# Bucketed attention and two expert stages on one core: the order of the queries, and the maxima over two PSUM banks

## The chip, the cores and the metric

The kernel runs on one core of a Trainium2 chip. The metric is the device time of one execution in microseconds (us); lower is better. TensorE (PE in the profile) multiplies matrices, its weight loads (PEld) overlap its multiplications, VectorE is DVE, ScalarE is ACT, GpSimd is POOL, and SyncE (SP) only issues DMAs here. PSUM, into which TensorE writes, has 8 banks of 512 fp32 numbers per partition.

## The reference

Three stages follow one another: an attention in which a query sees only the keys of its own bucket, a layer of 8 experts with one expert per token, and a dense layer with a gated product. Only the first matters here.

```python
def _attn_ref(q, k, v, proj):            # q, k, v: 2 x 8 x 768 x 64
    q_bits = einsum(q, proj) > 0         # 6 bits per row; the same for k
    mask = q_bucket == k_bucket
    scores = where(mask, q @ k.T / sqrt(D), -1e9)
    attn = exp(scores - max(scores)); attn /= attn.sum() + 1e-9
    return attn @ v
```

## The kernel before

**Layout.** There are 16 heads (2 batches of 8) of 768 queries and keys, NC = 6 chunks of P = 128 each; HS = 384 is half a head. Every engine gets its instructions in the order in which the program is written, and works through them in that order; a wait of one instruction holds all that stand behind it on its engine. For each head there is a set of four SBUF tiles X, Y, K1, K2 (`sets`, four sets in turn). X holds 64 rows of the scaled queries, 12 rows of bucket bits (64 to 75) and, in row 76, the maximum of each query; K2 holds the same for the keys, with -1 in row 76. Y and K1 hold the other halves of a split of the fp32 numbers. So one product of X and K2 over 77 rows gives score, mask and minus the maximum in one go.

**Steps.** The attention runs over 96 steps, one per head and chunk of keys. Step k does, in this order: the work that is due (`due(k - 0.5)`), a fp16 copy of the exponentials of the step before (`high`), `scores(k)` (four matmuls of 384 columns, L402 and L403, and two exponentials, L404), the rest of the split (`low`, mostly on GpSimd), the maxima of a chunk of queries eight steps ahead (`mx(k + 8)`), in every odd step the products with the values of two steps (`pv`, 36 matmuls, L430 to L432), and what else is due. `later` is a table of due times with the constants of `Q`: preparing a head (`prep`, about 13 steps ahead; its DMAs go through SP's queue), the bits of four heads (`bits`), scaling the values (`vmax`, `vscale`, `vsplit`), and dividing the finished sums (`evac`, at the begin of the step after a head's last `pv`; the next head's first `pv` ends the step after that one).

**Maxima.** `mx` multiplies a chunk of queries (the stationary operand, 76 rows and 128 columns of X) with all keys of K2, 384 columns at a time, each into a PSUM tile of one bank (`ps_m`, three tiles), and VectorE reduces each half to one number per query. The queries of chunk c are the columns c, c + 6, c + 12 and so on (`c::NC`), so that partition p gets queries 6p to 6p + 5. After the sixth chunk a reduction (L391) takes the larger half and -0.5 as a floor; `top[:, h]`, 128 partitions of 6 numbers, is then written by a DMA (L392) as 768 numbers into row 76 of X. The sixth chunk of head h is sent in step 6h - 3, and `scores(6h)` is the first that reads the row.

**Sums.** `pv` adds into a PSUM tile of one bank per head (`ps_v`, two tiles in turn). `scores` uses two banks (`ps_t`), small things one (`ps_x`): eight in all.

**Start.** Before step 0 the first head's bits are computed (two tiles of `ps_m`, L667), then its six chunks of maxima; after the sixth chunk the first two of the eight dot products for the bits of heads 0 to 3 (`bits(0)`, L358, into two tiles of `ps_v`), four filling matmuls (`heat`), the maxima of the values on VectorE (L514), a transposition for their scale (L531), the other dot products, and the first scores.

Of the kernel before, what the change touches and what calls it, by code (L numbers as in the profile page):

```python
# [9 lines left out]
F32 = mybir.dt.float32  # L10
F32R = mybir.dt.float32r
F16 = mybir.dt.float16
I32 = mybir.dt.int32
AF = mybir.ActivationFunctionType
# [37 lines left out]
def moe_attention_kernel(ctx, tc, qk, v, vt, pj, wg, w1, w2, win, wout, out, cap):  # L52
# [5 lines left out]
    def opened(stack, name, bufs, side="left", **kw):  # L58
        return stack.enter_context(tc.tile_pool(name=name, bufs=bufs, side=side, reuse_waits="tile", **kw))

    def f32(t):
        return t.bitcast(F32)
# [201 lines left out]
    with ExitStack() as actx:  # L264
# [2 lines left out]
        ph = opened(actx, "ph", 1)  # L267
        pt = opened(actx, "pt", 2)
        ps_t = opened(actx, "ps_t", 2, space=PSUM)
        ps_m = opened(actx, "ps_m", 3, space=PSUM)  # L270
        ps_v = opened(actx, "ps_v", 2, space=PSUM)
        ps_x = opened(actx, "ps_x", 1, space=PSUM)

        idle_sb = pa.tile([P, 512], F16, tag="idle", name="idle_sb")
# [15 lines left out]
        ]  # L290
        warm = pa.tile([1, 1], F32, tag="warm", name="warm")
        pool.memset(b3, 3.0)
        rt, b_t = {}, {}
        nm = pa.tile([P, NH, NC], F32, tag="nm", name="nm")
        top = pa.tile([P, NH, NC], F32R, tag="top", name="top")
        mxs = [pa.tile([P, NC, 3], F32, tag=f"mx{i}", name=f"mx{i}") for i in range(2)]
        for t in mxs:
            dve.memset(t[:, :, 2:3], -0.5)
        nflag = pa.tile([1, NH // 2 + 1], I32, tag="nflag", name="nflag")
        pf_t, phi_t, plo_t, pv_t, xp_t = {}, {}, {}, {}, {}  # L300
        vr_t, vt_t, vh_t, am_t, sc_t, sw_t = {}, {}, {}, {}, {}, {}
# [8 lines left out]
        def prep(h, first=False):  # L310

            st = sets[h % 4]
            r = rt[h]
            if h == 1:
                hi = pt.tile([P, S], F32, tag="pf", name=f"hi{h}", bufs=4).bitcast(F32R)
            else:
                hi = ph.tile([P, S], F32R, tag="hi", name=f"hi{h}", bufs=1)
            lo = ph.tile([P, S], F32R, tag="lo", name=f"lo{h}")
            act.activation(hi, r, AF.Copy, scale=SC)
            if not first:  # L320
                sp.dma_start(out=f32(st["X"])[0:D], in_=f32(hi)[0:D])
                sp.dma_start(out=f32(st["K2"])[0:D], in_=f32(hi)[D:P])
            if h == 1:
                yield
            sp.dma_start(out=f32(st["K1"])[0:D], in_=f32(hi)[D:P])
            sp.dma_start(out=f32(st["Y"])[D:P], in_=f32(hi)[0:D])
            yield
            if h > 2:
                put_bits(h)
            if h in Q["ap"]:  # L330
                x = pt.tile([P, S], F32, tag="pf", name=f"rs{h}", bufs=4) if h < 2 else r
                act.activation(x, r, AF.Copy, scale=SC)
                pool.tensor_tensor(out=lo, in0=x, in1=f32(hi), op=ALU.subtract)
            else:
                dve.scalar_tensor_tensor(out=lo, in0=r, scalar=SC, in1=f32(hi), op0=ALU.mult, op1=ALU.subtract)
            sp.dma_start(out=f32(st["K1"])[D:P], in_=f32(lo)[D:P])
            sp.dma_start(out=f32(st["Y"])[0:D], in_=f32(lo)[0:D])

        def put_bits(h):
            st = sets[h % 4]  # L340
            b = b_t[h // 4]
            o = 32 * (h % 4)
            sp.dma_start(out=f32(st["X"])[D : D + 12], in_=f32(b)[o : o + 12])
            sp.dma_start(out=f32(st["K2"])[D : D + 12], in_=f32(b)[o + 12 : o + 24])
# [34 lines left out]
        def mx(n):  # L379
            h, c = divmod(n, NC)  # L380
            st = sets[h % 4]
            mm = mxs[h % 2]
            for n in range(2):
                ps = ps_m.tile([P, 512], F32, tag="m", name=f"psm{h}{c}{n}")
                pe.matmul(  # L385
                    ps[:, :HS], st["X"][0:76, c::NC], st["K2"][0:76, n * HS : (n + 1) * HS], start=True, stop=True
                )
                dve.tensor_reduce(out=mm[:, c, n : n + 1], in_=ps[:, :HS], axis=AX.X, op=ALU.max)  # L388
            if c == NC - 1:

                dve.tensor_reduce(out=top[:, h], in_=mm, axis=AX.X, op=ALU.max)  # L391
                sp.dma_start(out=f32(st["X"])[76:77, :].rearrange("o (p c) -> o p c", c=NC), in_=f32(top)[:, h])  # L392

        def scores(k):
            h, j = divmod(k, NC)
            st = sets[h % 4]
            pf = pf_t[k] = pt.tile([P, S], F32, tag="pf", name=f"pf{k}", bufs=4)
            kc = slice(j * P, (j + 1) * P)
            for n in range(2):
                ps = ps_t.tile([P, 512], F32, tag="t", name=f"pst{k}{n}")  # L400
                qc = slice(n * HS, (n + 1) * HS)
                pe.matmul(ps[:, :HS], st["K1"][:, kc], st["Y"][:, qc], start=True, stop=False)  # L402
                pe.matmul(ps[:, :HS], st["K2"][0:77, kc], st["X"][0:77, qc], start=False, stop=True)  # L403
                act.activation(  # L404
                    pf.rearrange("k (c n p) -> k c n p", c=NC, n=2)[:, :, n],
                    ps[:, :HS].rearrange("k (p c) -> k c p", c=NC), AF.Exp, scale=0.125 / SC / SC,
                )

        def high(k, eng):
            phi_t[k] = pt.tile([P, S], F16, tag="phi", name=f"phi{k}", bufs=6)  # L410
# [252 lines left out]
        for n in range(2):  # L663
            for i, t in enumerate(("X", "K2")):
                c = slice(n * HS, (n + 1) * HS)
                ps = (ps_m, ps_t)[i].tile([P, 512], F32, tag="mt"[i], name=f"psf{n}{i}")
                pe.matmul(  # L667
                    ps[D : D + 12, :HS], pj_sb[i * D : (i + 1) * D, 12 * i : 12 * i + 12], r0[i * D : (i + 1) * D, c],
                    start=True, stop=True,
                )  # L670
                signs(st[t][D : D + 12, c], ps[D : D + 12, :HS], cst_sb[D : D + 12, i : i + 1])
# [4 lines left out]
        consts()  # L676
        pool.dma_start(out=xd[0:1, :], in_=zrow[:, :DM])
        DOT = (5,)
        b0 = bits(0, [ps_v.tile([P, 512], F32, tag="v", name=f"psb0{n}") for n in range(2)])
        for n in range(NC):  # L680
            mx(n)
            if n in DOT:
                next(b0)
        heat(ps_t, "t", Q["hn"][0])
        for i in range(4):
            vmax(0, i)
# [82 lines left out]
        for k in range(STEPS + LAG + 2):  # L769
            due(k - 0.5)  # L770
            if 0 < k <= STEPS and not on_dve(k - 1):
                high(k - 1, act)
            if k < STEPS:
                scores(k)
            if k < 8:
                heat(ps_v, "v", Q["hn"][1 + k])
            u = k - 2
            if 0 <= u < STEPS:
                if u not in phi_t:
                    high(u, dve)  # L780
                low(u, pool if on_pool(u) else dve)
            for n in AHEAD[k] if k < len(AHEAD) else (k + LEAD,):
                if n < STEPS:
                    mx(n)
            for u in (k - LAG - 1, k - LAG) if k % 2 else ():
                if 0 <= u < STEPS:
                    pv(u)
            due(k)
# [551 lines left out]
```

## Time and profile before

| | |
|---|---|
| time, median of 3 runs | 718.79 us (717.63 to 719.08) |
| the profiled execution, its own time | 712.88 us |
| its span, first to last instruction | 711.1 us |
| mean granted clock of TensorE | 0.983 |
| busy in the span: TensorE, VectorE | 682.9 us (96%), 503.5 us (71%) |
| busy in the span: ScalarE, GpSimd | 376.8 us (53%), 260.6 us (37%) |

The profiled execution is 5.9 us below the median of the timed runs. The attention takes about the first third of the span, from the first maxima at 7.74 us to the last exponentials near 234 us; the experts and the dense layer follow. A matmul's bar is longer than the distance to the next one, since matmuls are pipelined: how much of TensorE's time one takes is read from the starts of neighbours. A row that holds several instructions gives their count behind an x.

### The profile page before, as it was taken

The numbers are of one execution on the slowest core, as the hardware profiler recorded it, in microseconds if no ns is written. First come the engines' busy times: TensorE is split into PE (matmuls) and PEld (weight loads), VectorE is DVE, ScalarE is ACT, GpSimd is POOL, SyncE is SP. The second block draws the span as 40 slices with busy tenths as digits, with TensorE's granted clock in tenths as the row PEclk, the third lists the DMA queues.
The fourth block names the chain that finished last, engine by engine and source line by source line (L and its number), as shares of the span: only waits on it lengthen the run. The fifth ranks groups of instructions, "written<-read, shape, count | busy, mean of one in ns | idle before, by whom it ended". The sixth has DMA issues, their size and how long they took to land. (4 is left out here: it accounts for less than half of the span.)

```text
span 711.1 us, 14232 instructions
## 1 busy us (share of the span) xinstructions
PE 682.9 (96%) x5528; PEld 598.2 (84%) x5528; DVE 503.5 (71%) x988; ACT 376.8 (53%) x713; POOL 260.6 (37%) x202
## 2 busy tenths in 40 slices
PE   7999999999998699999999998999999999999996
PEld 2689898898897489999999996788888888888885
DVE  6778889889999788778777785888888632222320
ACT  3468869778779366655666642333333442223420
POOL 4347877977982411110110001333333423311212
PEclk8789999999999999999999999999999999999999
DMA  7585855746480376666665543234333000000001
GB/s 224 120 227 130 239 141 156 226 127 167 98 230 25 115 238 223 218 208 209 209 213 189 193 150 123 89 128 137 121 119 118 1 17 29 30 16 1 0 30 59
DMA packets 37841, 94.14 MB, mean 132 GB/s; under 512 B 7576, under 2 KB 13720, under 8 KB 37760
## 3 DMA queue, kind: packets, MB, share of 16 engines
q1 hardware_dynamic: 34672, 85.71, 40.2%
q0 software_dynamic: 2400, 7.36, 3.1%
q8 instruction: 46, 0.75, 0.4%
q14 instruction: 35, 0.29, 0.1%
q10 hardware_dynamic: 688, 0.03, 0.1%
HBM read 67.14 MB, written 6.29 MB: 103 GB/s over the span
## 5 line engine op out<-in xcount | busy, mean ns | idle before, releaser
L418 POOL TENSOR_TENSOR plo<-pf,phi 128x768 f16<-128x768 f32 x86 | 146.7, 1728 | 60.6 <-ACT phi L412 25.9
L996 POOL TENSOR_TENSOR ib<-wi,ia 128x512 fp32r<-128x512 f32 x32 | 50.1, 1566 | 230.1 <-ACT ia L995 230.1
L388 DVE TENSOR_REDUCE mx<-psm 128x1 f32<-128x384 f32 x192 | 96.3, 548 | 20.1 <-PE psm L385 19.8
L404 ACT ACTIVATE pf<-pst 128x384 f32<-128x384 f32 x192 | 83.4, 486 | 48.9 <-PE pst L403 47.5
L135 DVE TENSOR_TENSOR wl<-raw,wh 128x512 fp32r<-128x512 f32 x128 | 86.7, 688 | 10.2 <-ACT wh L134 3.7
L1223 ACT ACTIVATE rl<-psg,b 128x512 f32<-128x512 f32 x64 | 37.3, 582 | 94.6 <-PE psg L1221 94.5
L1221 PE MATMUL psg<-yTh,ia 128*128 128x512 f32 (+1 forms) x256 | 86.4, 338 | 0.7 <-DVE rl L1224 0.2
L1224 DVE SCALAR_TENSOR_TENSOR rl<-rl,psg 128x512 f32<-128x512 f32 x64 | 35.1, 550 | 73.3 <-ACT rl L1223 73.3
L1221 PE MATMUL psg<-yTh,ib 128*128 128x512 f32 (+1 forms) x256 | 85.9, 335 | 0.0
L1221 PE MATMUL psg<-yTl,ia 128*128 128x512 f32 (+1 forms) x256 | 85.7, 335 | 0.0
L134 ACT ACTIVATE wh<-raw 128x512 fp32r<-128x512 f32 x128 | 77.3, 623 | 2.1 <-issue 1.5
L1243 PE MATMUL pso<-cl,gh 128*128 128x512 f32 x192 | 76.7, 399 | 0.5 <-POOL cl L996 0.5
L402 PE MATMUL pst<-Y,K 128*128 128x384 f32 x192 | 75.1, 391 | 2.0 <-ACT pf L404 2.0
L1243 PE MATMUL pso<-ch,gl 128*128 128x512 f32 x192 | 75.5, 393 | 0.0
L1243 PE MATMUL pso<-ch,gh 128*128 128x512 f32 x192 | 75.5, 393 | 0.0
L412 ACT ACTIVATE phi<-pf 128x768 f16<-128x768 f32 x85 | 71.7, 844 | 1.9
L978 PE MATMUL psy<-hh,wh 128*128 128x224 f32 x256 | 71.3, 279 | 0.0
L385 PE MATMUL psm<-K,X 76*128 76x384 f32 x192 | 66.8, 429 | 4.3 <-DVE mx L388 3.5
L978 PE MATMUL psy<-hl,wh 128*128 128x224 f32 x256 | 70.2, 274 | 0.0
L978 PE MATMUL psy<-hh,wl 128*128 128x224 f32 x256 | 70.1, 274 | 0.0
L403 PE MATMUL pst<-X,K 77*128 77x384 f32 x192 | 66.2, 345 | 0.0
L432 PE MATMUL psv<-vh,plo 128*128 128x73 f16 x576 | 63.6, 196 | 1.7 <-DVE plo L418 1.7
(204 smaller groups left out, 1642.6 us busy)
## 6 DMA issues: line engine op xcount, KB each, us to landing
raw<-in_w_dram SPq DMA_DIRECT2D x64, 512.0 KB
rc<-in_win_dram SPq DMA_DIRECT2D x16, 512.0 KB
rc<-in_wout_dram SPq DMA_DIRECT2D x16, 512.0 KB
r<-in_qk_dram SPq DMA_DIRECT2D x16, 384.0 KB
K<-hi SPq DMA_DIRECT2D x31, 192.0 KB
vr<-in_v_dram SPq DMA_DIRECT2D x4, 768.0 KB
vt<-in_vt_dram SPq DMA_DIRECT2D x8, 384.0 KB
Y<-hi SPq DMA_DIRECT2D x16, 192.0 KB
```

The lines of the kernel that those rows point to most:

```text
L134: act.activation(wh[e, i][:, c], r, AF.Copy)
L135: lo.tensor_tensor(out=wl[e, i][:, c], in0=r, in1=f32(wh[e, i])[:, c], op=ALU.subtract)
L385: pe.matmul(ps[:, :HS], st["X"][0:76, c::NC], st["K2"][0:76, n * HS : (n + 1) * HS], start=True, stop=True)
L388: dve.tensor_reduce(out=mm[:, c, n : n + 1], in_=ps[:, :HS], axis=AX.X, op=ALU.max)
L402: pe.matmul(ps[:, :HS], st["K1"][:, kc], st["Y"][:, qc], start=True, stop=False)
L403: pe.matmul(ps[:, :HS], st["K2"][0:77, kc], st["X"][0:77, qc], start=False, stop=True)
L404: act.activation(pf.rearrange("k (c n p) -> k c n p", c=NC, n=2)[:, :, n], ps[:, :HS].rearrange("k (p c) -> k c p", c=NC), AF.Exp, scale=0 ...
L412: act.activation(phi_t[k], pf_t[k], AF.Copy)
L418: eng.tensor_tensor(out=plo_t[k], in0=pf_t.pop(k), in1=phi_t[k], op=ALU.subtract)
L978: pe.matmul(ps, l, r, start=n == 0, stop=n == 3 * KF - 1)
L1221: pe.matmul(ps, l, x, start=n == 0, stop=n == 3 * KD - 1)
L1243: pe.matmul(po[blk][s], l, r, start=first and n == 0, stop=last and n == 2)
```

## The change

The host lays the queries of a head out chunk by chunk: column 128c + p holds query 6p + c. Chunk c is now 128 neighbouring columns of X, and the exponentials are written in the order in which they are computed. `mx` writes all 768 columns (a matmul of 512 and one of 256) into a PSUM tile of two banks, which one VectorE instruction reduces. `ps_m` has two such tiles (four banks in place of three), and `ps_v` gives up one of its two. The maxima no longer lie in the order of row 76: `put_top`, in the step after the sixth chunk and behind that step's scores, transposes them on TensorE, copies the 6 x 128 numbers on VectorE, and a DMA writes them as six pieces of 128 numbers. The floor of -0.5 is a `tensor_scalar` in place of the reduction. `put_bits`, two DMAs, stands ahead of a head's other DMAs instead of behind four of them, from head 3 on. At the start the dot products of `bits(0)` go into a tile of `ps_m`.

```diff
--- before.py
+++ after.py
@@ -267,8 +267,8 @@
         ph = opened(actx, "ph", 1)
         pt = opened(actx, "pt", 2)
         ps_t = opened(actx, "ps_t", 2, space=PSUM)
-        ps_m = opened(actx, "ps_m", 3, space=PSUM)
-        ps_v = opened(actx, "ps_v", 2, space=PSUM)
+        ps_m = opened(actx, "ps_m", 2, space=PSUM)
+        ps_v = opened(actx, "ps_v", 1, space=PSUM)
         ps_x = opened(actx, "ps_x", 1, space=PSUM)
 
         idle_sb = pa.tile([P, 512], F16, tag="idle", name="idle_sb")
@@ -290,12 +290,10 @@
         ]
         warm = pa.tile([1, 1], F32, tag="warm", name="warm")
         pool.memset(b3, 3.0)
-        rt, b_t = {}, {}
+        rt, b_t, new = {}, {}, []
         nm = pa.tile([P, NH, NC], F32, tag="nm", name="nm")
         top = pa.tile([P, NH, NC], F32R, tag="top", name="top")
-        mxs = [pa.tile([P, NC, 3], F32, tag=f"mx{i}", name=f"mx{i}") for i in range(2)]
-        for t in mxs:
-            dve.memset(t[:, :, 2:3], -0.5)
+        mxs = [pa.tile([P, NC], F32, tag=f"mx{i}", name=f"mx{i}") for i in range(2)]
         nflag = pa.tile([1, NH // 2 + 1], I32, tag="nflag", name="nflag")
         pf_t, phi_t, plo_t, pv_t, xp_t = {}, {}, {}, {}, {}
         vr_t, vt_t, vh_t, am_t, sc_t, sw_t = {}, {}, {}, {}, {}, {}
@@ -316,6 +314,8 @@
             else:
                 hi = ph.tile([P, S], F32R, tag="hi", name=f"hi{h}", bufs=1)
             lo = ph.tile([P, S], F32R, tag="lo", name=f"lo{h}")
+            if h > 2:
+                put_bits(h)
             act.activation(hi, r, AF.Copy, scale=SC)
             if not first:
                 sp.dma_start(out=f32(st["X"])[0:D], in_=f32(hi)[0:D])
@@ -325,8 +325,6 @@
             sp.dma_start(out=f32(st["K1"])[0:D], in_=f32(hi)[D:P])
             sp.dma_start(out=f32(st["Y"])[D:P], in_=f32(hi)[0:D])
             yield
-            if h > 2:
-                put_bits(h)
             if h in Q["ap"]:
                 x = pt.tile([P, S], F32, tag="pf", name=f"rs{h}", bufs=4) if h < 2 else r
                 act.activation(x, r, AF.Copy, scale=SC)
@@ -380,16 +378,22 @@
             h, c = divmod(n, NC)
             st = sets[h % 4]
             mm = mxs[h % 2]
-            for n in range(2):
-                ps = ps_m.tile([P, 512], F32, tag="m", name=f"psm{h}{c}{n}")
-                pe.matmul(
-                    ps[:, :HS], st["X"][0:76, c::NC], st["K2"][0:76, n * HS : (n + 1) * HS], start=True, stop=True
-                )
-                dve.tensor_reduce(out=mm[:, c, n : n + 1], in_=ps[:, :HS], axis=AX.X, op=ALU.max)
+            ps = ps_m.tile([P, 1024], F32, tag="m", name=f"psm{h}{c}")[:, 0:S]
+            for k in (slice(0, 512), slice(512, S)):
+                pe.matmul(ps[:, k], st["X"][0:76, c * P : (c + 1) * P], st["K2"][0:76, k], start=True, stop=True)
+            dve.tensor_reduce(out=mm[:, c : c + 1], in_=ps, axis=AX.X, op=ALU.max)
             if c == NC - 1:
 
-                dve.tensor_reduce(out=top[:, h], in_=mm, axis=AX.X, op=ALU.max)
-                sp.dma_start(out=f32(st["X"])[76:77, :].rearrange("o (p c) -> o p c", c=NC), in_=f32(top)[:, h])
+                dve.tensor_scalar(out=top[:, h], in0=mm, scalar1=-0.5, scalar2=None, op0=ALU.max)
+                new.append(h)
+
+        def put_top(h):
+
+            ps = ps_m.tile([P, 1024], F32, tag="m", name=f"psx{h}")
+            pe.transpose(ps[0:NC, 0:P], f32(top)[:, h], ident)
+            row = ph.tile([NC, P], F32R, tag="row", name=f"row{h}", bufs=2)
+            dve.tensor_copy(row, ps[0:NC, 0:P])
+            sp.dma_start(out=f32(sets[h % 4]["X"])[76:77, :], in_=f32(row))
 
         def scores(k):
             h, j = divmod(k, NC)
@@ -401,10 +405,7 @@
                 qc = slice(n * HS, (n + 1) * HS)
                 pe.matmul(ps[:, :HS], st["K1"][:, kc], st["Y"][:, qc], start=True, stop=False)
                 pe.matmul(ps[:, :HS], st["K2"][0:77, kc], st["X"][0:77, qc], start=False, stop=True)
-                act.activation(
-                    pf.rearrange("k (c n p) -> k c n p", c=NC, n=2)[:, :, n],
-                    ps[:, :HS].rearrange("k (p c) -> k c p", c=NC), AF.Exp, scale=0.125 / SC / SC,
-                )
+                act.activation(pf[:, qc], ps[:, :HS], AF.Exp, scale=0.125 / SC / SC)
 
         def high(k, eng):
             phi_t[k] = pt.tile([P, S], F16, tag="phi", name=f"phi{k}", bufs=6)
@@ -663,7 +664,7 @@
         for n in range(2):
             for i, t in enumerate(("X", "K2")):
                 c = slice(n * HS, (n + 1) * HS)
-                ps = (ps_m, ps_t)[i].tile([P, 512], F32, tag="mt"[i], name=f"psf{n}{i}")
+                ps = (ps_m, ps_t)[i].tile([P, (1024, 512)[i]], F32, tag="mt"[i], name=f"psf{n}{i}")
                 pe.matmul(
                     ps[D : D + 12, :HS], pj_sb[i * D : (i + 1) * D, 12 * i : 12 * i + 12], r0[i * D : (i + 1) * D, c],
                     start=True, stop=True,
@@ -676,11 +677,13 @@
         consts()
         pool.dma_start(out=xd[0:1, :], in_=zrow[:, :DM])
         DOT = (5,)
-        b0 = bits(0, [ps_v.tile([P, 512], F32, tag="v", name=f"psb0{n}") for n in range(2)])
+        ps0 = ps_m.tile([P, 1024], F32, tag="m", name="psb0")
+        b0 = bits(0, [ps0[:, 512 * n : 512 * (n + 1)] for n in range(2)])
         for n in range(NC):
             mx(n)
             if n in DOT:
                 next(b0)
+        put_top(new.pop())
         heat(ps_t, "t", Q["hn"][0])
         for i in range(4):
             vmax(0, i)
@@ -772,6 +775,8 @@
                 high(k - 1, act)
             if k < STEPS:
                 scores(k)
+            if new:
+                put_top(new.pop())
             if k < 8:
                 heat(ps_v, "v", Q["hn"][1 + k])
             u = k - 2
@@ -1303,6 +1308,7 @@
     from concourse.bass_utils import run_bass_kernel_spmd
 
     q, k, v = inputs["q"], inputs["k"], inputs["v"]
+    q = q.reshape(B, H, P, NC, D).transpose(0, 1, 3, 2, 4).reshape(B, H, S, D)
     qk = np.concatenate([q.transpose(0, 1, 3, 2), k.transpose(0, 1, 3, 2)], axis=2).reshape(NH, P, S)
     vv = v.reshape(NH, NC, P, D).transpose(2, 0, 1, 3).reshape(P, NH * NC * D)
     vt = v.reshape(NH // 2, 2, S, D).transpose(0, 1, 3, 2).reshape(NH // 2, P, S)
```

## Rows read from the trace of the kernel before

**Rows 1.** Stretches: length, busy us (count) of PE, PEld, DVE, ACT, POOL; clock, DMA.

```profile
42.00:180.00 138.00, 135.80 (x1641) 121.77 (x1638) 119.06 (x271) 109.54 (x203) 107.26 (x70) 1.00 0.64 172
180.00:222.00 42.00, 41.04 (x529) 37.73 (x526) 39.10 (x92) 33.72 (x65) 32.74 (x23) 1.00 0.49 136
7.00:18.00 11.00, 10.26 (x24) 4.76 (x27) 9.11 (x21) 0.94 (x2) 6.18 (x19) 0.69 0.84 226
```

**Rows 2.** Groups of TensorE weight loads by shape: total, mean ns of one, idle before.

```profile
L385 PEld LDWEIGHTS psm<-K,X 76*128 76x128 f32 x192 | 53.3, 313 | 11.8 <-DVE mx L388 8.3 <-ACT hi L319 2.1 <-issue 0.8
...
L403 PEld LDWEIGHTS pst<-X,K 77*128 77x128 f32 x192 | 37.1, 193 | 0.0
```

**Rows 3.** Timeline of TensorE, head 9's begin: start, length in us, instruction, count.

```profile
144.07 0.34 PE L403 MATMUL pst<-X,K 77*128 77x384 f32 x1
...
146.11 0.21 PE L430 MATMUL psv<-vh,phi 128*128 128x73 f16 x1
...
147.59 0.34 PE L403 MATMUL pst<-X,K 77*128 77x384 f32 x1
...
147.95 0.34 PE L403 MATMUL pst<-X,K 77*128 77x384 f32 x1
148.13 0.62 PE L385 MATMUL psm<-K,X 76*128 76x384 f32 x2
...
148.86 0.34 PE L403 MATMUL pst<-X,K 77*128 77x384 f32 x1
...
149.41 0.61 PE L385 MATMUL psm<-K,X 76*128 76x384 f32 x2
149.86 0.21 PE L430 MATMUL psv<-vh,phi 128*128 128x73 f16 x1
```

**Rows 4.** Timeline of TensorE in the last stage, matrices of 512 and 256 columns.

```profile
442.05 0.39 PE L1221 MATMUL psg<-yTl,ia 128*128 128x512 f32 x1
442.28 0.28 PE L1221 MATMUL psg<-yTh,ia 128*128 128x256 f32 x1
442.40 0.28 PE L1221 MATMUL psg<-yTh,ib 128*128 128x256 f32 x1
```

**Rows 5.** Waits of TensorE from 30 to 360 us: total, times, longest.

```profile
PE psm L385 <- DVE mx L388: 1.9, 7, 0.4
```

**Rows 6.** Groups of VectorE instructions by shape.

```profile
L388 DVE TENSOR_REDUCE mx<-psm 128x1 f32<-128x384 f32 x192 | 96.3, 548 | 20.1 <-PE psm L385 19.8
```

**Rows 7.** Timeline of VectorE around head 9's begin.

```profile
135.69 1.94 DVE L388 TENSOR_REDUCE mx<-psm 128x1 f32<-128x384 f32 x4
...
144.58 0.61 DVE L448 TENSOR_TENSOR xp<-psv,rd 128x432 f32<-128x432 f32 x1
```

**Rows 8.** Timeline of the start, TensorE and VectorE.

```profile
7.74 5.60 PE L385 MATMUL psm<-K,X 76*128 76x384 f32 x12 [0.78 <-DVE X L347]
...
8.30 5.67 DVE L388 TENSOR_REDUCE mx<-psm 128x1 f32<-128x384 f32 x12 [0.18 <-PE psm L385]
...
13.27 2.77 PE L358 MATMUL psb<-r,pj_sb 128*32 128x384 f32 x4
...
14.10 1.92 DVE L514 TENSOR_REDUCE am<-vr 128x1 f32<-128x384 f32 x4
...
16.13 0.22 DVE L525 TENSOR_REDUCE am<-wg_sb 128x1 f32<-128x64 f32 x1
...
17.65 0.27 PE L531 MATMUL psn<-ident,am 128*2 128x128 f32 x1
...
19.28 0.44 PE L402 MATMUL pst<-Y,K 128*128 128x384 f32 x1
```

**Rows 9.** Timeline of SyncE's queue: DMA issues.

```profile
194.58 0.51 SPq L392 DMA_DIRECT2D X<-top  x1
...
201.22 0.81 SPq L343 DMA_DIRECT2D X<-b  x1
```

**Rows 10.** Timeline of TensorE at head 13's begin.

```profile
198.03 0.34 PE L403 MATMUL pst<-X,K 77*128 77x384 f32 x1
```

## The prediction

> **What bounds the kernel now.** I read the stretches first, then the weight loads, then the timeline of one step, and the start by itself. In the stretches [rows 1] the reader is to see that TensorE is busy for 135.8 of the 138 us from 42 to 180 us, at the full clock (2.4 GHz), while VectorE has 119.1, ScalarE 109.5 and GpSimd 107.3. So TensorE sets the pace there. From 180 to 222 us VectorE has 39.1 of 42 us as well: two engines bound that stretch. The later stages use nothing of what is changed, and move as a block.
>
> What TensorE spends on a chunk of maxima is read from starts in the timeline, not from bars. From one L403 to the next across a chunk (148.13 to 148.86) pass 0.73 us, of which one L402 takes 0.18, as the next start behind 147.95 shows: a chunk that scores follow costs 0.55 us. One that `pv` follows costs 0.45 us (149.41 to 149.86) [rows 3]. The weight loads tell why: 313 ns for L385, whose 128 columns lie six numbers apart, against 193 ns for L403 with neighbouring columns and one row more [rows 2].
>
> **The change part by part.**
>
> *Neighbouring columns for the chunk's weights, 512 + 256 columns.* With plain loads a matmul of 512 columns takes 0.23 us from start to start, and one of 256 columns 0.12 [rows 4]: 0.35 us. That is 0.20 us less where scores follow and 0.10 where `pv` follows. 82 chunks are sent one per step from step 6 to step 87, half of each kind: 41 x 0.20 + 41 x 0.10 = **12.3 us** less of TensorE. The Trainium skill's page "TensorE: Matmul & The Clock Gate" (Step-by-step: what each phase is for) speaks against it: the next weights load while a matmul runs, and a load's time goes by its number of columns. By that the sum would have 0 here in place of 12.3; it is a rival below, and the 313 ns and the 0.55 us disagree with it.
>
> *One reduction over 768 numbers.* Two of 384 cost 0.93 us in a stream: (1.94 - 0.55) / 3 = 0.46 each [rows 6, 7]. Between 64 numbers in 0.22 us [rows 8] and 384 in 0.55, a number costs 1.03 ns, so 768 take 0.94 us alone and 0.86 in a stream; at worst twice 0.55. I take 0.86: 96 x 0.07 = 6.7 us less of VectorE, and the copy of the row (128 numbers by the same line, 0.29 us) gives 16 x 0.29 = 4.6 back. VectorE then has about 117 us in the first stretch, and TensorE's time falls towards it; cover remains. The floor replaces a reduction of a similar size: 0.
>
> *Two tiles of two banks.* A tile now holds a chunk, so TensorE may run two chunks ahead, not one and a half. It waits 1.9 us for VectorE's maxima so far [rows 5]; the bounds are 0 and 1.9 less, and I take **1.0 us** less.
>
> *`put_top`: transposition.* 15 heads (head 0 belongs to the start). The transposition L531 of the trace takes 0.27 us alone [rows 8], and 256 columns at a stride of 0.12 us bound 128 columns from above in a stream; between 0.05 and 0.27, I take 0.12: **1.8 us** more (0.8 to 4).
>
> *`put_top`: the row's way.* The transposition waits in TensorE's queue for VectorE's floor, with the chunk and the `pv` of its step behind it; the copy waits on VectorE, and behind it the reductions; SP's DMA goes one step later than L392 did, and behind it stand the DMAs of the head after next. The reader is `scores(6h)`. For head 9 TensorE is done with the scores of step 52 at 144.07 + 0.18, and reads the row at 147.59 [rows 3]: 3.34 us, less 0.30 for two cheaper chunks, plus 0.12 for the transposition: 3.16. Needed are 0.27 + 0.29 + the DMA, so there is no wait if that takes 2.6 us or less from issue to use. No row shows its landing; head 13's was issued at 194.58 and used at 198.03 with no wait [rows 9, 10], which bounds it by 3.45 us. So 0 to 0.85 us a head, 0 to 12.8 us in all. I take 0.2, nearer to nothing since 3.45 is a bound with an unknown slack, and six pieces replace 128: **3.0 us** more. By the fixed cost of about 2.0 us that the Trainium skill's page "DMA: Bandwidth & Descriptors" (Anatomy of one DMA) gives for a transfer, an estimate would be no wait at all, and a sum 3.0 us lower.
>
> *One tile for the sums.* A head's first `pv` must now wait for the division of the head before. That ends at 144.58 + 0.61 = 145.19, the `pv` starts at 146.11 [rows 3, 7]: 0.92 us of cover, of which 0.30 - 0.12 go. Price 0; if the division came 1 us later, 0.3 us a head.
>
> *`put_bits` earlier.* Two issues of 0.81 us [rows 9] pass the four DMAs of `hi` in SP's queue; these wait for ScalarE anyway, some 12 steps before use. 0. The exponentials keep count and size, and ScalarE has 28 us to spare in the first stretch: 0.
>
> *The second stretch.* TensorE's gain there, some 20 chunks or 3 us, meets a VectorE with 2.9 us free. I give half back: **1.5 us**.
>
> *The start.* `bits(0)` now holds one of the two `ps_m` tiles until its last dot product, so the six first chunks share the other: product, reduction, product. Before, a reduction started every 0.46 us, and all were through at 8.30 + 5.67 = 13.97, 6.2 us after the first matmul at 7.74. After, a chunk takes 0.56 (7.74 to 8.30) + 0.23 for the second matmul + 0.94 + a hand-over: 1.75 us, and six 10.5: 4.3 us later. At half the clock (1.2 GHz; the mean granted in this stretch is 0.69 [rows 1]) the matmuls add about 0.25 each time, 5.8 in all. The dot products stand behind the sixth chunk, the row's transposition behind them, and the values' maxima on VectorE (1.92 us) behind the row's copy: 2.77 + 0.27 + 0.29 + 1.92 + 0.3 = 5.5 us to the transposition L531, which came 17.65 - 13.27 = 4.4 us after the dot products' begin [rows 8]: up to 1.1 more. So 4.3 to 6.9 us, and the first scores, at 19.28 so far, hide none of it, as all later work stands behind them. I take **5.0 us**.
>
> **Sum.** -12.3 - 1.0 + 1.8 + 3.0 + 1.5 + 5.0 = **-2.0 us**: a span of 709.1 instead of 711.1. The profiled execution (712.88 us) lies below the median of the runs, 718.79; I take the difference over: **716.8 us**.
>
> **The rivals.**
> 1. *The row comes late, and it gets slower.* At 0.7 us a head, the wait at `scores(6h)` costs 10.5 instead of 3.0: +5.5, 724.3 us. It decides from 0.33 us a head on (5.0 in all). For it: the way has three hand-overs in place of one, and begins a step later. Against: head 13's bound.
> 2. *All goes well.* No wait for the row, 0.8 for the transpositions, the 1.9 of waits gone, nothing given back late, 4.3 at the start: -12.3 - 1.9 + 0.8 + 4.3 = -9.1, 709.7 us.
> 3. *VectorE takes over.* With about 117 of 130 us it stops TensorE here and there; if 2 us more are lost so, start and gain cancel: 718.8 us, no change. For it: its 39.1 of 42 in the second stretch.
> 4. *The weight loads were hidden all the while*, so the chunks gain nothing: the sum without 12.3 and without the 1.5 given back, +8.8, 727.6 us. Against it stand the starts in [rows 3].
>
> **How the numbers follow.** Forecast 0.43, rival 1 0.21, rival 2 0.16, rival 3 0.17, rival 4 0.03. A change of 0.2% (1.4 us) is about what a measurement of this kernel can tell from none. Alone, the forecast's bounds (start 4.3 to 6.9, transpositions 0.8 to 4, waits 0 to 1.9) reach from 714 to 719.5, most of it faster. With most of rival 2 and rival 1 the range is 709.5 to 724.5. Faster: most of the forecast and rival 2, 0.53; same: most of rival 3 and the forecast's upper end, 0.20; slower: 0.27.
>
> **What the profile after would show.** Weight loads of L385's successor near 193 ns, and a chunk at 0.35 us between its neighbours' starts; a reduction near 0.94 us; the first scores near 24 us instead of 19.28; first L403 of a head without a wait for the row's DMA, or with one of some tenths; first `pv` of a head without a wait for the division. I am wrong if the first scores come at 20 or 27, if waits for the row exceed 0.33 us a head, or if the granted clock between 18 and 42 us differs much from before, since that stretch has work that goes by it.

## The result, and the profile after

| | before | after |
|---|---|---|
| time, median of 12 runs each | 716.81 us (712.92 to 719.08) | 724.33 us (721.68 to 729.24) |
| span of the profiled execution | 711.1 us | 726.3 us |

The ratio after to before is 1.0126, with a 95% interval of 1.0103 to 1.0148: slower by 0.0126 x 716.8 = 9.0 us (7.5 by the medians), where 2.0 us faster were forecast. The two profiled executions lie further apart, 728.01 us by the time of after's own against 712.88: the traces show where time goes, the ratios how much.

The stretches after, as [rows 1]:

```profile
42.00:180.00 138.00, 130.06 (x1559) 107.54 (x1560) 112.67 (x199) 104.18 (x191) 102.48 (x68) 0.96 0.61 160
180.00:222.00 42.00, 39.76 (x439) 34.40 (x436) 36.46 (x62) 29.57 (x55) 28.77 (x20) 0.87 0.57 147
7.00:18.00 11.00, 8.90 (x21) 3.98 (x20) 7.16 (x11) 1.05 (x2) 6.29 (x19) 1.00 0.82 210
```

TensorE is busy for 5.7 us less between 42 and 180 us, but got less done: 82 matmuls fewer stand in the same time. It waits, and its mean granted clock is 0.96 and 0.87 in the first two stretches, where it was 1.00.

Groups by shape, as [rows 2, 6]:

```profile
L383 PEld LDWEIGHTS psm<-K,X 76*128 76x128 f32 x192 | 36.5, 208 | 13.1 <-DVE mx L384 5.5 <-issue 3.7 <-DVE row L395 2.6
L384 DVE TENSOR_REDUCE mx<-psm 128x1 f32<-128x768 f32 x96 | 89.8, 949 | 22.4 <-PE psm L383 21.8
```

The weight load is down from 313 to 208 ns and the reduction takes 949 ns, as forecast (193 ns, 0.94 us).

One pair of steps, head 9's first, as [rows 3]:

```profile
155.24 0.34 PE L407 MATMUL pst<-X,K 77*128 77x384 f32 x1
...
156.50 0.34 PE L407 MATMUL pst<-X,K 77*128 77x384 f32 x1
...
158.91 0.34 PE L407 MATMUL pst<-X,K 77*128 77x384 f32 x1
```

The step with scores behind its chunk takes 1.26 us from first L407 to first L407; before it took 147.59 to 148.86 = 1.27 [rows 3]. The step with `pv` takes 2.41; before it took 2.50, from 148.86 to the next first L403:

```profile
151.36 0.34 PE L403 MATMUL pst<-X,K 77*128 77x384 f32 x1
```

So the first kind got nothing.

The waits of TensorE, 30 to 360 us, as [rows 5]:

```profile
PE psb L356 <- DMA r<-in_qk_dram: 4.2, 3, 1.6
PE pst L407 <- DMA X<-row: 3.8, 2, 3.2
...
PE psm L383 <- DVE row L395: 1.8, 2, 1.2
...
PE psm L383 <- DVE mx L384: 0.7, 3, 0.2
```

VectorE's maxima hold TensorE for 0.7 us instead of 1.9. The three longest of the waits that are new are for the loads of `r`, for the row's DMA, and of a chunk for the row's copy, whose transposition sits in one of the two `ps_m` tiles.

The first of them starts in SyncE's queue. Head 4's row and what stands behind it, before and after (DMA issues):

```profile
76.43 0.51 SPq L392 DMA_DIRECT2D X<-top  x1
76.99 2.14 SPq L308 DMA_DIRECT2D r<-in_qk_dram  x4
```

```profile
80.04 0.77 SPq L396 DMA_DIRECT2D X<-row  x1
80.86 2.68 SPq L306 DMA_DIRECT2D r<-in_qk_dram  x4
```

The row's DMA waits for its copy with the four loads of the heads 8 to 11 behind it, so these start 3.9 us later, while head 4 itself comes only 0.8 us later. The dot products then wait (L356, 4.2 us in the waits above), and behind such waits the clock is lower (TensorE's timeline, then two stretches, columns as in [rows 1]):

```profile
89.64 0.83 PE L356 MATMUL psb<-r,pj_sb 128*32 128x384 f32 x2 [1.58 <-DMA r<-in_qk_dram]
```

```profile
83.00:104.00 21.00, 17.98 (x166) 12.51 (x165) 12.37 (x23) 10.88 (x21) 11.54 (x10) 0.84 0.57 156
186.00:205.00 19.00, 16.91 (x158) 14.61 (x156) 14.69 (x25) 11.45 (x22) 14.57 (x9) 0.73 0.33 80
```

A mean of 0.84 and 0.73 means that part of each stretch ran at the lower level, 1.2 GHz. Head 4's first L407 stands at 82.56 us and head 5's at 102.81, a head of 20.25 us; before it was 81.80 to 95.66, 13.86 us.

In the second of these stretches one waits for the other: the transposition (L393) for the floor, the copy (L395) behind other work of VectorE, a chunk (L383) for the copy (VectorE, TensorE and SyncE's queue at head 12):

```profile
188.84 1.41 DVE L387 TENSOR_SCALAR top<-mx 128x6 fp32r<-128x6 f32 x1
...
190.17 1.74 DVE L178 SCALAR_TENSOR_TENSOR sc<-dl,rank 128x48 f32<-128x48 f32 x1
190.40 0.27 PE L393 MATMUL psx<-ident,top 128*6 128x128 f32 x1 [0.30 <-DVE top L387]
...
192.82 0.27 DVE L395 CAST row<-psx 6x128 fp32r<-6x128 f32 x1
...
193.12 0.75 SPq L396 DMA_DIRECT2D X<-row  x1
193.15 0.62 PE L383 MATMUL psm<-K,X 76*128 76x512 f32 x2 [1.19 <-DVE row L395]
```

From the floor's start to the row's issue pass 4.28 us; before, the two stood 0.2 us apart.

The start, as [rows 8]:

```profile
9.38 1.82 DVE L384 TENSOR_REDUCE mx<-psm 128x1 f32<-128x768 f32 x2 [1.16 <-PE psm L383]
...
14.51 2.77 PE L356 MATMUL psb<-r,pj_sb 128*32 128x384 f32 x4 [0.19 <-DVE mx L384]
...
17.62 0.28 DVE L395 CAST row<-psx 6x128 fp32r<-6x128 f32 x1 [2.10 <-PE psx L393]
...
21.76 0.45 PE L406 MATMUL pst<-Y,K 128*128 128x384 f32 x1
```

The reductions come in pairs: both tiles serve the first chunks, and `psb0` takes its tile only at the first dot product. The first scores are 2.5 us later than before, not 5. About half of this is the row's way: VectorE waits 2.10 us for the transposition, with the values' maxima behind the copy, and from the first dot product to the transposition for the values' scale pass 5.6 us (14.51 to 20.12) instead of 4.4. In experiment 5 below, without the row's transposition and copy, the first scores start at 19.85, 0.6 us later than before, with a mean clock of 0.69 between 7 and 18 us as before.

### The profile page after: what moved, and what is told of

Same layout as the page of the kernel before. It is cut to its first block, busy times and chain, and to the rows that moved or that the text cites. A ratio compares the mean times of both kernels' runs of the same rounds, so it can differ in the third digit from the quotient of the medians.

```text
span 726.3 us, 14208 instructions
## 1 busy us (share of the span) xinstructions
PE 687.4 (95%) x5544; PEld 589.4 (81%) x5544; DVE 509.3 (70%) x906; ACT 378.5 (52%) x713; POOL 261.3 (36%) x202
## 5 line engine op out<-in xcount | busy, mean ns | idle before, releaser
L384 DVE TENSOR_REDUCE mx<-psm 128x1 f32<-128x768 f32 x96 | 89.8, 949 | 22.4 <-PE psm L383 21.8
L406 PE MATMUL pst<-Y,K 128*128 128x384 f32 x192 | 77.3, 403 | 2.0 <-ACT pf L408 2.0
L407 PE MATMUL pst<-X,K 77*128 77x384 f32 x192 | 68.2, 355 | 3.8 <-DMA X<-row 3.8
L433 PE MATMUL psv<-vh,plo 128*128 128x73 f16 x576 | 67.1, 200 | 1.7 <-DVE plo L419 1.7
L431 PE MATMUL psv<-vh,phi 128*128 128x73 f16 x576 | 67.8, 203 | 0.0
```

The lines of the kernel that those rows point to most:

```text
L384: dve.tensor_reduce(out=mm[:, c : c + 1], in_=ps, axis=AX.X, op=ALU.max)
L431: pe.matmul(o, hi[:, cc], vv[:, j, 0:VA], start=j == 0 and c == 0, stop=False, **grp)
```

## The experiments

All ratios are to the kernel before, run on the same chip in turn. Theories at first: (Q) the row's DMA in SyncE's queue, (F) the floor, (R) the row's longer way, (C) chunks that never gained.

**1. Loads earlier: `e1_r_early`.**

```diff
-            at(max(0, 24 * (h // 4 - 1) - 2) + h % 4 / 4, load_r, h)
+            at(max(0, 24 * (h // 4 - 1) - 5) + h % 4 / 4, load_r, h)
```

> The changed kernel with the loads of queries and keys of heads 8 to 15 issued three steps earlier, ahead of the row's DMA in SyncE's queue. Queue theory (the row's DMA waits in SyncE's queue for the transposition and the copy, and holds the loads behind it back; TensorE then stands idle before the dot products of the bits, and its clock falls): no wait of the dot products L356 for a load, head 4 to head 5 takes 13 to 14 us instead of 20.3, no stretch at half the clock near 92 us, and the time falls by 5 to 7 us to a ratio of 1.002 to 1.006. Rival (the loads are late because the DMA engines are busy, or the stall is one of PSUM tiles): the stall stays or moves, ratio 1.010 to 1.015.

Measured: 728.71 us, ratio 1.0183 (1.0158 to 1.0207). Slower than the change alone, and above both expectations. The dot products no longer wait, but the reading of the row does, 10.8 us at four heads against 3.8 at two (SyncE's queue at head 4):

```profile
78.05 2.56 SPq L306 DMA_DIRECT2D r<-in_qk_dram  x4
81.90 0.78 SPq L396 DMA_DIRECT2D X<-row  x1
```

The edit turned the order round: the loads are ahead, and the row arrives behind them. The collision is real, but shifting the loads does not remove it.

**2. The floor as a reduction again: `e2_floor_reduce`.** A fixed column of -0.5 stands beside each maximum.

```diff
-                dve.tensor_scalar(out=top[:, h], in0=mm, scalar1=-0.5, scalar2=None, op0=ALU.max)
+                dve.tensor_reduce(out=top[:, h], in_=mm, axis=AX.X, op=ALU.max)
```

> The changed kernel with the floor of -0.5 taken by a reduction over two columns, as before, in place of the tensor_scalar. Floor theory (the tensor_scalar is stretched while GpSimd works, the reduction is not): 0.17 us each instead of 0.63 in the mean, VectorE 7 us less busy, the row of heads 11 to 14 comes earlier, and the time falls by 1 to 4 us, ratio 1.007 to 1.011. Rival (the stretched floor lies beside other work): floor 0.17 us, but the time stays, ratio 1.012 to 1.014.

Measured: 721.22 us, 1.0077 (1.0050 to 1.0103), 0.0049 below the change, 3.5 us (1.0 to 6.0 by the two intervals). F holds, for a part. The line's view gives minimum, median and maximum in ns, for the change and for this run:

```profile
L387 DVE TENSOR_SCALAR top<-mx x16: 170/497/1430, 15.4 to 234.2; 128x6 fp32r<-128x6 f32 x16
```

```profile
L389 DVE TENSOR_REDUCE top<-mx x16: 166/166/168, 15.0 to 226.1; 128x6 fp32r<-128x12 f32 x16
```

**3. The row in the floor's own step: `e3_row_same_step`.** `put_top` moves from behind the next step's scores to the end of the sixth chunk's step.

```diff
-            if new:
-                put_top(new.pop())
             if k < 8:
...
                 if 0 <= u < STEPS:
                     pv(u)
+            if new:
+                put_top(new.pop())
             due(k)
```

> The changed kernel with the transposition, the copy and the row's DMA at the end of the step of the sixth chunk, behind its products with the values, in place of behind the scores of the next step. Queue theory: SyncE is free 0.7 to 1.5 us earlier at each head, the dot products of head 4 to 5 wait 1 to 2 us less, time down by 1 to 3 us, ratio 1.008 to 1.011. Row theory (the waits of the scores for the row's landing make the loss): waits for the row, 3.8 us so far, fall below 2, time down by 2 us at most. If TensorE must wait for the floor instead, the time stays or rises.

Measured: 737.01 us, 1.0306 (1.0271 to 1.0341), the worst of all. TensorE stands in front of the transposition until the floor is done: that wait (psx, L393, for top, L387) comes 14 times, 16.1 us in all and 3.0 at the longest.

**4. The three together: `e4_all_three`.**

> All three edits: loads earlier, floor by a reduction, row in the same step. If queue and floor together make the loss, the gain of the cheaper chunks is left: 0.3 us for each pair of steps, 12 us, less some 3 at the start and 2 for transpositions, so 4 to 8 us below the kernel before, ratio 0.989 to 0.995. If the loss has another cause (one buffer for the sums, two tiles for the maxima, waits on VectorE), ratio 1.000 or more.

Measured: 729.40 us, 1.0195 (1.0167 to 1.0222). With the short floor the transposition's wait falls from 16.1 to 6.1 us. That is still more than is saved of the waits in experiment 2: those for the row fall from 7.8 to 4.7 us and those for the loads from 1.2 to nothing, 4.3 us in all.

**5. The old way of the row: `e5_old_row`.** Experiment 2, and the row goes straight from `top` by a DMA behind the floor, without transposition and copy. In this run and the next the row's numbers stand with other queries.

```diff
-                new.append(h)
+                put_top(h)
...
-            ps = ps_m.tile([P, 1024], F32, tag="m", name=f"psx{h}")
-            pe.transpose(ps[0:NC, 0:P], f32(top)[:, h], ident)
-            row = ph.tile([NC, P], F32R, tag="row", name=f"row{h}", bufs=2)
-            dve.tensor_copy(row, ps[0:NC, 0:P])
-            sp.dma_start(out=f32(sets[h % 4]["X"])[76:77, :], in_=f32(row))
+            sp.dma_start(out=f32(sets[h % 4]["X"])[76:77, :].rearrange("o (p c) -> o p c", c=NC), in_=f32(top)[:, h])
```

> The changed kernel with the floor by a reduction, and with the row's way of before: no transposition and no copy, the DMA issued in the step of the sixth chunk, 24 bytes from each partition. This leaves the reordering out, so that row 76 holds the maxima in another order than the queries. Row theory (what is lost comes from the longer way of the row alone: it collides with the loads in one queue): no wait of the scores for the row above 1 us in all, no wait of the dot products for loads, and the time falls to that of the kernel before less the gain of the steps with values, 41 x 0.1 us, plus 2 us at the start: ratio 0.993 to 1.001. Rival (two-bank tiles, one buffer for the sums or the early bits cost it): ratio 1.005 or more.

Measured: 708.41 us, 0.9888 (0.9851 to 0.9926). R holds: with the old way of the row and a reduction as floor, all the rest of the change is a gain of 8.0 us (5.3 to 10.7 by the interval). That is more than the expectation (0.993 to 1.001) reckoned with; the part on why the prediction was wrong comes back to it.

**6. The old way in the new place: `e10_old_row_late`.** Experiment 5, but `put_top` is called where the change calls it, a step later.

> The changed kernel with the floor as a reduction, the row written straight from the maxima (no transposition, no copy; its numbers then stand with other queries), but issued where the changed kernel issues it, a step later in the order. If the loss is the length of the row's way (2 to 4 us from the floor to the issue of the DMA against 0.2 us): the issue comes soon after the floor all the same, and the ratio is 0.987 to 0.994 as with the old place. If the place in SyncE's order is what costs: loads and bit rows are held again, ratio 1.000 to 1.008.

Measured: 713.57 us, 0.9954 (0.9929 to 0.9979): between the two expectations. At most heads the row is issued 0.2 us behind the floor as in experiment 5. At head 1 it is not: here it stands behind two copies of `lo` that wait for VectorE, there ahead of them (SyncE's queue, this run and then experiment 5):

```profile
35.09 0.53 SPq L336 DMA_DIRECT2D K<-lo  x1
...
36.31 0.60 SPq L394 DMA_DIRECT2D X<-top  x1
```

```profile
33.06 0.53 SPq L394 DMA_DIRECT2D X<-top  x1
...
34.31 0.55 SPq L336 DMA_DIRECT2D K<-lo  x1
```

Waits of TensorE for the row are 7.7 us in two places, against 1.1 in experiment 5: 4.6 us at head 1, and 3.1 at head 14, where the row is issued 0.2 us behind the floor but right behind three loads of 512 KB, so that this part is not the order's. The profiled execution took 719.32 us, 5.8 above the median of its run; it shows where, and the ratio how much. By the ratios the place in the order costs 0.0066, 4.7 us (1.5 to 7.9).

**7. The row on ScalarE's queue: `e6_row_on_act`.** Experiment 2 with another queue.

```diff
-            sp.dma_start(out=f32(sets[h % 4]["X"])[76:77, :], in_=f32(row))
+            act.dma_start(out=f32(sets[h % 4]["X"])[76:77, :], in_=f32(row))
```

> The changed kernel with the floor by a reduction, and with the row's DMA issued from ScalarE's queue instead of SyncE's, so that the loads neither stand behind it nor ahead of it in one queue. Queue theory: no wait of the dot products for loads, waits of the scores for the row below 2 us (7.8 with the reduction alone), time 3 to 7 us below that of the reduction alone, ratio 0.998 to 1.004. If the DMA engines themselves are full, the row is late all the same: waits for the row stay near 8 us, ratio 1.006 to 1.010. ScalarE now waits for the copy with the next exponentials behind it: up to 0.5 us a head, 7 us, against it.

Measured: 725.77 us, 1.0131 (1.0090 to 1.0172); slower than experiment 2 and above both expectations, a miss. SyncE no longer holds the loads, so they start at 74.60, and head 4's row behind them; head 9's row has no loads ahead (DMA issues and the readers):

```profile
74.60 1.45 SPq L308 DMA_DIRECT2D r<-in_qk_dram  x3
...
78.22 0.68 ACTq L398 DMA_DIRECT2D X<-row  x1
...
83.37 0.44 PE L409 MATMUL pst<-X,K 77*128 77x384 f32 x1 [2.47 <-DMA X<-row]
...
152.66 0.68 ACTq L398 DMA_DIRECT2D X<-row  x1
...
155.35 0.45 PE L409 MATMUL pst<-X,K 77*128 77x384 f32 x1 [0.25 <-DMA X<-row]
```

5.15 us from issue to use with the loads ahead (5.61 at head 8), 2.69 without (at head 5 as well), all ended by the row. In experiment 1, on SyncE's queue behind these loads, it is 6.78 and 6.18. So a queue of its own saves some of it, but does not save a small transfer from loads in flight. The Trainium skill says so on its page "DMA: Bandwidth & Descriptors" (Issuing engines are not separate DMA queues): all queues end on the same 16 engines. The trace agrees with its 5.15 us against 2.69. ScalarE, too, stands 6.7 us in front of the row's copy in this run, with exponentials behind; how much of the time this is, and how much the loads, no run parts.

**8. The same with the loads earlier: `e11_row_act_loads`.** Experiments 1 and 7 on top of 2.

> The run with the row's DMA on ScalarE's queue, and the loads of the heads from 8 on issued three steps earlier. Theory of the full DMA engines (the row's 3 KB stand behind 2.3 MB of loads in the engines, whatever queue they are issued from): with the loads gone by, the rows of heads 4 and 8 land 2.7 to 3.2 us after their issue and not 5.1 and 5.6 us; some 5 us less, ratio 1.002 to 1.008. If the cost was ScalarE's own delay of the issue, or the loads still stand before the row, nothing is gained: 1.010 to 1.018.

Measured: 727.64 us, 1.0127 (1.0079 to 1.0176). The second expectation, but it does not test the theory: on SyncE's queue only the row stood between the two places, so with the row gone the loads were issued just as far ahead of it, from 76.36 us against a row at 79.98.

**9. Six DMAs in place of the transposition: `e12_row_by_chunk`.** Experiment 5 with the row in the right order.

```diff
...
+            if c % 3 == 2:
+                dve.tensor_reduce(out=top[:, h, c - 2 : c + 1], in_=mm[:, c - 2 : c + 1], axis=AX.X, op=ALU.max)
+                for i in range(c - 2, c + 1):
+                    sp.dma_start(out=f32(st["X"])[76:77, i * P : (i + 1) * P], in_=f32(top)[:, h, i : i + 1])
```

> The changed kernel without transposition and copy, its row in the right order: the floor is a reduction over three chunks at a time, and each chunk's 128 maxima go by a DMA of their own into their 128 places of the row, three DMAs after the third chunk and three after the sixth. It adds 80 DMA issues of 0.5 us on SyncE, which are two thirds of them ahead of nothing late. If the loss was the transposition, the copy and the wait for them: last row number lands some 1.5 us issue and 2 us transfer after the last floor, inside the 4.0 to 5.1 us that the run with the old way had; ratio 0.987 to 0.997. If the issues hold SyncE's queue, or the pieces of 4 bytes land later than 4 us: the scores wait for the row again, ratio 1.000 to 1.015.

Measured: 732.62 us, 1.0236 (1.0193 to 1.0280), above both expectations. TensorE waits 11.7 us for the row in seven places. The way needs no transposition and no copy, but it fills the queue: three issues together take 1.8 to 2.4 us there, twice a head. Whether pieces of 4 bytes also land late was not separated.

**10. A third bank for the scores, in the kernel before: `e7_before_pst3`.** It tests C: if the step of 1.27 us is set by scores, exponential and the return of one of two `ps_t` banks, a third bank shortens it, and the cheaper chunk cannot.

```diff
-        ps_t = opened(actx, "ps_t", 2, space=PSUM)
+        ps_t = opened(actx, "ps_t", 3, space=PSUM)
...
-        ps_v = opened(actx, "ps_v", 2, space=PSUM)
+        ps_v = opened(actx, "ps_v", 1, space=PSUM)
```

> The kernel before with three banks for the scores and one for the sums of the values (the start's dot products in the maxima's tiles), nothing else. Score-bank theory (a step followed by scores is set by product, exponential, release of one of two banks, 1.26 us, not by the chunk's weight loads): such a step falls from 1.27 to between 1.07 and 1.17 us, and the time falls, ratio 0.985 to 0.998. Rival (the weight loads set it): the step stays at 1.27 and the ratio at 0.998 to 1.002. If one buffer for the sums costs something, the time rises and the products with the values wait for the division.

Measured: 715.18 us, 0.9978 (0.9946 to 1.0009). The time lies on the border of the two expectations and decides nothing; the step, shown with the next experiment, falls to 1.17 us.

**11. The new layout with that third bank: `e8_layout_pst3`.** Experiment 2, with one-bank halves in three `ps_m` banks, reduced one by one as before.

> The changed kernel's layout, transposition and queue order with the floor by a reduction, but the maxima in halves of one bank as before, and three banks for the scores. Score-bank theory: now a chunk's cheaper loads show, the step followed by scores falls to 1.07 to 1.12 us; the row's way still collides with loads and gets tighter, so 2 to 6 us less than with the reduction alone, ratio 0.998 to 1.005. Rival: the step stays at 1.26, ratio 1.006 to 1.012.

Measured: 723.76 us, 1.0086 (1.0048 to 1.0124): the rival's ratio, though the steps are those of the score-bank theory (first reading of X in head 9, TensorE's timeline: experiment 10, then 11):

```profile
147.80 0.34 PE L403 MATMUL pst<-X,K 77*128 77x384 f32 x1
...
148.97 0.34 PE L403 MATMUL pst<-X,K 77*128 77x384 f32 x1
...
151.46 0.34 PE L403 MATMUL pst<-X,K 77*128 77x384 f32 x1
```

```profile
159.40 0.34 PE L411 MATMUL pst<-X,K 77*128 77x384 f32 x1
...
160.45 0.34 PE L411 MATMUL pst<-X,K 77*128 77x384 f32 x1
...
162.82 0.34 PE L411 MATMUL pst<-X,K 77*128 77x384 f32 x1
```

With three banks the step with scores falls from 1.27 to 1.17 us, and with the new layout besides to 1.05. So C holds for the step: the chunk's saving is there, but with two score banks it ends in a wait for the exponential. That it can be had as time is not shown. Experiment 10 gained 1.6 us (-0.6 to 3.9) where 41 x 0.10 would be 4.1, and this run is no faster than experiment 2 (1.0077), with the same way of the row: TensorE's waits for VectorE's maxima are 8.5 us at 14 places here, 2.4 at 7 there.

**12. The two-bank tile alone: `e9_two_banks`.** The kernel before, its layout and its row, with the two-bank tile, the one reduction and one tile for the sums.

```diff
-            for n in range(2):
-                ps = ps_m.tile([P, 512], F32, tag="m", name=f"psm{h}{c}{n}")
...
-                dve.tensor_reduce(out=mm[:, c, n : n + 1], in_=ps[:, :HS], axis=AX.X, op=ALU.max)
+            ps = ps_m.tile([P, 1024], F32, tag="m", name=f"psm{h}{c}")[:, 0:S]
+            for k in (slice(0, 512), slice(512, S)):
+                pe.matmul(ps[:, k], st["X"][0:76, c::NC], st["K2"][0:76, k], start=True, stop=True)
+            dve.tensor_reduce(out=mm[:, c, 0:1], in_=ps, axis=AX.X, op=ALU.max)
```

> The kernel before with only the two-bank tile and its one reduction (a chunk's 768 scores in two banks, one buffer for the sums of the values, the floor as a fixed column of the final reduction); queries interleaved as before, the row written straight from the maxima as before. Theory A, the 0.1 us of each step with products of the values comes from the cheaper weight loads of the new layout: those steps stay at 2.50 us, only VectorE's waits and the short head starts go, ratio 0.992 to 0.999. Theory B, the gain lies in the two-bank tile alone: 2.40 us a step and the ratio of the run with the old way of the row, 0.986 to 0.992.

Measured: 712.71 us, 0.9958 (0.9928 to 0.9987): a version that computes all of the reference and beats both kernels. The weight loads and the `pv` step, this run and then experiment 5 (head 9):

```profile
L385 PEld LDWEIGHTS psm<-K,X 76*128 76x128 f32 x192 | 51.7, 316 | 9.2 <-DVE mx L386 4.7 <-issue 2.9 <-DVE rd L441 1.3
...
146.79 0.34 PE L401 MATMUL pst<-X,K 77*128 77x384 f32 x1
...
149.27 0.34 PE L401 MATMUL pst<-X,K 77*128 77x384 f32 x1
```

```profile
L385 PEld LDWEIGHTS psm<-K,X 76*128 76x128 f32 x192 | 35.4, 197 | 9.9 <-DVE mx L386 6.5 <-issue 3.2
...
141.16 0.33 PE L405 MATMUL pst<-X,K 77*128 77x384 f32 x1
...
143.56 0.34 PE L405 MATMUL pst<-X,K 77*128 77x384 f32 x1
```

2.48 us with columns six apart, 2.40 with neighbours. So the layout gives 0.08 us of a `pv` step, 41 x 0.08 = 3.3 us in all, and the tile 0.02: theory A for the step. By the ratios the tile and what goes with it are 3.0 us of the 8.0 of experiment 5 (0.9 to 5.2), and the layout with the earlier `put_bits` the other 5.0 (1.6 to 8.4). By the rule on the Trainium skill's page "TensorE: Matmul & The Clock Gate" (Step-by-step: what each phase is for) the two kinds of weight load would take the same time; the 316 and 197 ns disagree.

## Why the prediction was wrong

Three steps of the prediction failed: the price of `put_top` (1.8 + 3.0 forecast, 13.5 measured), the floor at 0 (3.5 measured), and the chunk term (12.3 forecast, some 4 found in the steps). The ratios make a ladder from before to after, in us of 716.8; each step is the difference of two runs, uncertain by some 3 us, and the first three runs are from three chips, each with the kernel before on the same chip.

| step | ratios | us |
|---|---|---|
| layout, two-bank tile, the rest of the change | 1 to 0.9888 | -8.0 |
| the row's DMA a step later in the order | to 0.9954 | +4.7 |
| the transposition and the copy | to 1.0077 | +8.8 |
| the floor as a `tensor_scalar` | to 1.0126 | +3.5 |

**The rest of the change** was forecast at -12.3 - 1.0 + 1.5 + 5.0 = -6.8, against -8.0 measured. That the two are close is luck, since the terms were off against each other. The chunk term failed in its larger part: 41 x 0.10 = 4.1 us for `pv` steps is there (2.50 to 2.40), and 41 x 0.20 = 8.2 us for the others is not (1.27 to 1.26). The prediction took the 0.73 us from the chunk's start to the next L403, not from one L403 to the next as it says, less one L402, and put all of the 0.55 down to the chunk; [rows 3] hold only TensorE's starts, and what the L402 after the chunk waited for was not asked. Before, a step without any chunk, near the end, shows it:

```profile
219.08 0.34 PE L403 MATMUL pst<-X,K 77*128 77x384 f32 x1
...
220.07 0.45 PE L402 MATMUL pst<-Y,K 128*128 128x384 f32 x1 [0.29 <-ACT pf L404]
220.35 0.35 PE L403 MATMUL pst<-X,K 77*128 77x384 f32 x1
```

1.27 us too; a second one, at 226.60, takes 1.21. The start was priced at 5.0 and takes 0.6 in experiment 5, since both tiles serve it; of the 2.5 in the change the rest is the row's way. The 1.5 of the second stretch no run measures alone.

The `pv` steps and the start make -4.1 + 0.6 = -3.5 of the -8.0. In the traces most of what is left falls into the first head, which takes 19.15 us in experiment 5 (20.13 to 39.28) and 22.81 before (19.57 to 42.38): between 24 and 42 us the mean clock is 0.81 there, against 0.62 before, and 115 matmuls stand where there were 81. No term of the prediction stood for this. It is not this execution alone: over all runs the granted clock has a mean of 0.986 in experiment 5 and of 0.981 in the kernel before on the same chip. Why it is higher, and how much of the 8.0 us it makes, stays open. Of the prediction's signs of being wrong this is the one that came: between 18 and 42 us the clock is 0.93 in the change, where it was 0.72.

**The transposition and the row's way** failed by size and by kind: 1.8 + 3.0 were forecast, 4.7 + 8.8 came. The prediction asked if the row is in time for its reader. In this trace it mostly is: only 3.8 us of waits name it, 3.2 of them at head 1, and at heads 5 and 9 the row is used 1.98 us after its issue without a wait, inside the 2.6 us that the prediction asked for. What it didn't price is what the row holds up: the loads behind it in SyncE's queue, the chunk that waits for the transposition's `ps_m` tile, and the lower clock after TensorE has stood still. The prediction named these places ("behind it stand the DMAs of the head after next") and put no price on them. Rival 1 gave 724.3 us, close to the median, by a wait at `scores(6h)` that is the lesser part; its number is a coincidence.

**The floor** was priced at 0, as "a reduction of a similar size". It cost 3.5 us.

**Right** were the weight loads, the reduction, the copy (0.27 us), TensorE's waits for VectorE (1.0 less forecast, 1.9 to 0.7 measured) and the single tile for the sums: no wait after names its division, and in experiments 5 and 9 one of 0.5 and one of 0.4 us do. Rival 4 fell as a whole, since `pv` steps did gain; that the chunk gains nothing in the other half of the steps, because these wait for the exponential and not because the loads were hidden, was no rival.

Open: the 8.8 us are the transposition, the copy, the tile they hold, the DMA's other form (at head 4 issued in 0.77 us, before in 0.51) and the clock together; no run parts them.

## What to carry to other kernels

Before a saving on an engine is multiplied by its steps, look for a step that lacks the work and see if it is shorter; where it is not, something else sets the step. A shorter step is not yet a shorter kernel: experiment 11 has the shortest steps of all and gains no time by them. A small transfer that is moved later in an in-order queue costs what waits behind it, not only its own reader; and a scratch tile taken from a pool of two holds up the pool's main user. Keep a tiny instruction in the form that the trace has already shown.

## What the runs showed of the hardware

The floor's length goes with GpSimd's work. One of the long ones, with the instruction of GpSimd beside it:

```profile
122.55 1.65 POOL L419 TENSOR_TENSOR plo<-pf,phi 128x768 f16<-128x768 f32 x1
123.25 0.98 DVE L387 TENSOR_SCALAR top<-mx 128x6 fp32r<-128x6 f32 x1
```

It ends with GpSimd's instruction: 124.23 and 124.20 us. So do all twelve of the 16 floors that take longer than 0.2 us: each ends 0.02 to 0.03 us behind an instruction of GpSimd. The other four have none beside them and take 0.17 us. The reduction of six pairs takes 166 to 168 ns all 16 times, and twelve of these run beside a `plo`. The Trainium skill's page "SBUF — State Buffer" (SBUF: two separate sides) has a rule for this: VectorE, in a mode that uses two ports, and GpSimd share a pair of ports, and who starts first has it for the whole instruction. The trace agrees, with ends 0.02 to 0.03 us apart; that the floor runs in such a mode is not shown by it.
